# Renumbered column tiles and reordered products in a fused GEGLU feed-forward kernel

## The chip, the cores and the metric

The kernel runs on one core of a Trainium2 chip. The metric is device time in microseconds (us) of one execution. The kernel before took 276.17 us (median of 3 runs, 275.99 to 276.23).

Engines: PE is TensorE's matmul, PEld its weight load (it overlaps PE), DVE is VectorE, ACT is ScalarE, POOL is GpSimd, SP is SyncE, which here only issues transfers.

## The reference

```python
def _gelu(x):
    return jax.nn.gelu(x, approximate=True)

# x: (32, 32, 1024), w_gate and w_up: (1024, 3584), w_down: (3584, 1024), all bf16
def reference(x, w_gate, w_up, w_down):
    return (_gelu(x @ w_gate) * (x @ w_up)) @ w_down
```

As matrices: 1024 tokens, 1024 features, 3584 hidden columns, which are 28 column tiles of 128.

## The kernel before

The kernel lowers the number of matmuls with a seven-product scheme for 2 x 2 block matrices. The four blocks of the moving operand are halves of the tokens and halves of the contraction. The two column blocks of the weights are a "left" and a "right" tile, and there are 13 such pairs (two left-over tiles are computed directly at the start). Products 1 and 2 of a pair use plain weights and inputs (bf16). Products 3 to 7 use sums that DVE, POOL and ACT prepare, in fp32r; the profile prints their type as f32, and this text says fp32. A product is four matmuls of 128 x 512 for gate and four for up.

Four stages follow one another on PE:

- the start: 128 direct bf16 matmuls, fed by the first loads;
- four early pairs, whose products 1 and 2 were already done in the start, so each has 40 fp32 matmuls;
- nine later pairs, each with 16 bf16 and 40 fp32 matmuls;
- seven sweeps for the down projection, in the same scheme.

The program is a list of operations. PE keeps the order in which they are written. The other engines are sorted by the estimate `at`, and semaphores are added by dependence. One helper emits all operations, so nearly every operation has the same line in the profile (L117).

```python
        NX, F0 = 2, 11
        ...
        def load_first(eng, j, k0, k1, after=()):
            dma(eng, first[:, j, k0:k1, :], w_r[j][:, k0:k1, F0 * P:(F0 + 4) * P], 0, f"w0_{j}_{k0}", after)
        ...
        LEFT = [11, 12] + list(range(11))
        NP, EARLY = len(LEFT), 4

        def left(p): return LEFT[p]
        def right(p): return LEFT[p] + 15
        ...
        A, E, B, C = (0, 1), (2, 3), (4, 5), (6, 7)      # PSUM banks
        for p in range(NP):
            ...
            if p < EARLY:
                o = -4
                for j in range(2):
                    act(bank(B[j]), kept[p][:, j, :], COPY, at(0.1 + j * 0.1))
                product(5, 0, E[0], True)
                act(p5[0], bank(E[0]), COPY, at(1))
                product(5, 1, E[1], True)
                product(6, 0, B[0], False)
                act(bank(C[0]), bank(B[0]), COPY, at(3))
                act(p5[1], bank(E[1]), COPY, at(3.1))
                product(6, 1, B[1], False)
                act(bank(C[1]), bank(B[1]), COPY, at(4))
            else:
                o = 0
                product(1, 0, A[0], True)
                act(bank(B[0]), bank(A[0]), COPY, at(1))
                product(1, 1, A[1], True)
                act(bank(B[1]), bank(A[1]), COPY, at(2))
                product(5, 0, E[0], True)
                act(p5[0], bank(E[0]), COPY, at(3))
                product(2, 0, A[0], False)
                act(g11, bank(A[0]), GELU, at(4))
                product(2, 1, A[1], False)
                glu(ml, 0, g11, bank(A[1]), at(5.2))
                product(6, 0, B[0], False)
                act(bank(C[0]), bank(B[0]), COPY, at(6))
                product(6, 1, B[1], False)
                act(bank(C[1]), bank(B[1]), COPY, at(7))
                product(5, 1, E[1], True)
                act(p5[1], bank(E[1]), COPY, at(8))
            ...
            product(7, 0, C[0], False)        # adds to the copy in bank C
            ...
            product(3, 0, B[0], False)
            product(7, 1, C[1], False)
            product(3, 1, B[1], False)
            product(4, 0, C[0], False)
            product(4, 1, C[1], False)
```

`product(n, j, bank, start)` is half a product (j = 0 gate, j = 1 up), four matmuls of about 0.9 us together. In the text, "product 6" before "product 7" means these halves.

## Time and profile before

| stage, from the trace of before | us |
|---|---|
| up to the first fp32 matmul | 33.60 |
| early pairs (first to last matmul start) | 36.75 |
| later pairs (up to the last fp32 matmul start) | 113.46 |
| first two sweeps (bf16) | 24.23 |
| other sweeps, to the last matmul start | 63.45 |
| last matmul and stores | 3.25 |
| span | 274.73 |

The page of the profile says at once which engine to read. These are parts 1 and 4 of the page (busy time and share of the span; the chain of work that ended last) and two lines of part 5 (count, busy us, mean ns of one, idle time before):

```profile
span 274.7 us, 3245 instructions
PE 269.5 (98%) x1186; PEld 187.4 (68%) x1200; DVE 189.8 (69%) x221; ACT 126.1 (46%) x195; POOL 45.5 (17%) x27
...
PE 96%; DMA 2%; issue 0%; DVE 0%; ACTq 0%
...
L117 PEld LDWEIGHTS ps<-S,T 128*128 128x128 f32 x520 | 97.4, 188 | 22.7 <-issue 0.8
...
L117 PEld LDWEIGHTS ps<-arena 128*128 128x128 bf16 x272 | 24.7, 98 | 34.7 <-issue 4.5
```

PE is busy all the time and is the chain. "Busy" cannot show a small loss, since matmuls overlap (each is recorded as about 390 ns long, and the next starts after 216 or 227 ns); what counts is the distance from one matmul's start to the next. The trace has 1186 of 1200 matmuls here, so some blocks below read x7 for 8 or x15 for 16; the distance across a lost record is simply doubled. The instructions of PE in order of time, merged, show one later pair (start us, duration us, what):

```profile
96.01 1.67 PE L117 MATMUL ps<-arena 128*128 128x512 bf16 x7
97.34 1.27 PE L117 MATMUL ps<-S,T 128*128 128x512 f32 x4
98.45 1.90 PE L117 MATMUL ps<-arena 128*128 128x512 bf16 x8
100.00 8.55 PE L117 MATMUL ps<-S,T 128*128 128x512 f32 x36
108.62 1.67 PE L117 MATMUL ps<-arena 128*128 128x512 bf16 x7
```

The pair lasts 108.62 - 96.01 = 12.61 us, and goes from bf16 to fp32 twice. Single distances in the trace, in ns, around the second of these returns:

```
bf16 216, 217 | 27, 419, 229, 233, 236, 224, 231, 236, 228, 233, 231 | 226, 227, 227, 226
```

The steady distance is 216 ns for bf16 and 226.7 ns for fp32. The 27 and 419 belong together (the start of the first fp32 matmul is recorded early). After them nine matmuls are out of rhythm, 224 to 236 ns apart and on the whole late. Without such losses a pair would take 40 x 226.67 + 16 x 216 = 12,523 ns. It takes 12,607.

The early pairs lose in another way. ACT's instructions in order of time around the second early pair (the bracket gives idle time of ACT before, and what ended it):

```profile
44.88 0.58 ACT L117 ACTIVATE tmp<-ps 128x512 f32<-128x512 f32 x1
45.92 0.58 ACT L117 ACTIVATE ps<-ps 128x512 f32<-128x512 f32 x1 [0.46 <-PE ps L117]
46.42 0.59 ACT L117 ACTIVATE tmp<-ps 128x512 f32<-128x512 f32 x1
```

The middle line is the copy from bank B to bank C. It starts when product 6 ends and ends at 46.505 us; product 7's first matmul, which adds to the copy, starts at 46.650. The distances on PE there are 227, 226, 247, 306, 229, 233, 236 ns: 247 up to product 7's first matmul, 306 from it to the second. So PE is held up here in every early pair.

### The profile page before, as it was taken

To read this page: it belongs to the slowest core of one execution; us is meant where nothing else is said; L and a number is where in the kernel's file an instruction comes from. 1 tells how busy PE (TensorE), PEld (TensorE's weight loads), DVE (VectorE), ACT (ScalarE), POOL (GpSimd) and SP (SyncE) were. 2 spreads that over 40 slices of the span, in tenths; PEclk is the share of its full clock that TensorE was granted. 3 is DMA by queue.
4 is the path that set the end of the run, shared out by engine and by line. 5 is a ranking of instruction groups with operands and counts; after the bars stand their busy time and mean duration, and the time that the engine had idled before them with its cause. 6 is when DMAs were issued, how large, how long until landed. Compare 5 with 4: busy or idle time off the path is not lost.

```text
span 274.7 us, 3245 instructions
## 1 busy us (share of the span) xinstructions
PE 269.5 (98%) x1186; PEld 187.4 (68%) x1200; DVE 189.8 (69%) x221; ACT 126.1 (46%) x195; POOL 45.5 (17%) x27
## 2 busy tenths in 40 slices
PE   8999999999999999999999999999999999999995
PEld 4344478888686767767686867674447888888884
DVE  1039978988566657384655666579971999999942
ACT  2333766577455555556464555531120112255561
POOL 1000031134160605234150606000000000000000
PEclk9999999999999999999999999999999999999999
DMA  7999502962900830092500007097011000001112
GB/s 172 236 229 297 138 9 72 276 221 73 232 2 0 219 86 2 18 288 59 96 2 0 0 0 252 17 301 237 0 38 38 0 2 0 0 0 61 38 57 76
DMA packets 46863, 26.42 MB, mean 96 GB/s; under 512 B 12544, under 2 KB 46848, under 8 KB 46848
## 3 DMA queue, kind: packets, MB, share of 16 engines
q1 hardware_dynamic: 44624, 24.25, 32.5%
q10 hardware_dynamic: 2224, 1.97, 3.1%
q8 instruction: 9, 0.15, 0.2%
q14 instruction: 6, 0.05, 0.1%
HBM read 22.28 MB, written 2.10 MB: 89 GB/s over the span
## 4 chain that ended last, share of the span: by engine, by line
PE 96%; DMA 2%; issue 0%; DVE 0%; ACTq 0%
PE ps L117 96%; DMA arena<-in_w_up_dram 2%; DVE arena L117 0%; ACTq L117 0%
## 5 line engine op out<-in xcount | busy, mean ns | idle before, releaser
L117 PE MATMUL ps<-S,T 128*128 128x512 f32 x520 | 125.5, 398 | 0.0
L117 PEld LDWEIGHTS ps<-S,T 128*128 128x128 f32 x520 | 97.4, 188 | 22.7 <-issue 0.8
L117 POOL TENSOR_TENSOR T<-arena 128x1024 fp32r<-128x1024 bf16 x21 | 44.8, 2151 | 123.4 <-DVE T L117 114.7
L117 DVE TENSOR_TENSOR hT<-tmp,ps 128x512 bf16<-128x512 f32 x56 | 37.2, 686 | 39.2 <-PE ps L117 36.8
L117 ACT ACTIVATE tmp<-ps 128x512 f32<-128x512 f32 x64 | 38.2, 597 | 56.4 <-PE ps L117 56.4
L117 PE MATMUL ps<-arena 128*128 128x512 bf16 x261 | 60.7, 381 | 1.5 <-DMA arena<-in_w_up_dram 0.6
L117 ACT ACTIVATE ps<-ps 128x512 f32<-128x512 f32 x52 | 30.3, 584 | 48.4 <-PE ps L117 48.4
L117 PE MATMUL ps<-T,S 128*128 128x512 f32 x224 | 51.3, 390 | 0.0
L117 DVE TENSOR_TENSOR T<-arena,T 128x1024 fp32r<-128x1024 bf16 x40 | 48.5, 1219 | 0.0
L117 PEld LDWEIGHTS ps<-arena 128*128 128x128 bf16 x272 | 24.7, 98 | 34.7 <-issue 4.5
L117 PEld LDWEIGHTS ps<-T,S 128*128 128x128 f32 x224 | 42.1, 188 | 8.8
L117 DVE TENSOR_TENSOR tmp<-ps,tmp 128x512 f32<-128x512 f32 x26 | 18.0, 692 | 21.9 <-PE ps L117 21.9
L117 DVE TENSOR_TENSOR T<-arena 128x1024 fp32r<-128x1024 bf16 x19 | 22.7, 1222 | 7.5 <-PE ps L117 7.4
L117 PE MATMUL ps<-arena,hT 128*128 128x512 bf16 x109 | 24.0, 379 | 0.2
L117 DVE TENSOR_TENSOR ps<-ps,tmp 128x512 f32<-128x512 f32 x30 | 20.9, 696 | 2.8 <-PE ps L117 2.8
L117 PEld LDWEIGHTS ps<-arena,hT 128*128 128x128 bf16 x112 | 10.9, 98 | 13.2 <-issue 0.3
L117 ACT ACTIVATE tmp<-tmp 128x512 f32<-128x512 f32 x26 | 16.4, 632 | 5.8 <-DVE tmp L117 4.6
L117 DVE TENSOR_TENSOR S<-hT 128x1024 fp32r<-128x1024 bf16 x14 | 16.6, 1221 | 0.0
L117 ACT ACTIVATE T<-arena 128x1024 fp32r<-128x1024 bf16 x13 | 13.7, 1053 | 0.0
L117 PE MATMUL ps<-S 128*128 128x512 f32 x56 | 12.9, 389 | 0.0
L117 PEld LDWEIGHTS ps<-S 128*128 128x128 f32 x56 | 10.5, 188 | 2.2
L117 ACT ACTIVATE S<-arena 128x1024 fp32r<-128x1024 bf16 x9 | 9.3, 1056 | 3.1 <-PE ps L117 3.0
(25 smaller groups left out, 62.1 us busy)
## 6 DMA issues: line engine op xcount, KB each, us to landing
arena<-in_w_down_dram SPq DMA_DIRECT2D x4, 1792.0 KB, 9.3
arena<-in_w_gate_dram SPq DMA_DIRECT2D x10, 512.0 KB, 5.7
arena<-in_w_up_dram SPq DMA_DIRECT2D x10, 512.0 KB, 6.6
out_dram<-arena SPq DMA_DIRECT2D x12, 128.0 KB, 1.7
arena<-in_w_gate_dram SPq DMA_DIRECT2D x4, 256.0 KB, 4.9
arena<-in_w_up_dram SPq DMA_DIRECT2D x4, 256.0 KB, 5.0
arena<-in_w_up_dram ACTq DMA_DIRECT2D x4, 128.0 KB, 5.1
arena<-in_w_gate_dram ACTq DMA_DIRECT2D x2, 256.0 KB, 5.5
```

What stands on the lines that cost most here:

```text
L117: ins = name(eng, *args, **kw) if callable(name) else getattr(eng, name)(*args, **kw)
```

## The change

The intent: all weight transfers should begin at multiples of 512 bytes, and the second products (product 2) of a pair should run last, next to the first products of the following pair, so that bf16 matmuls stand together. The early pairs get a new order as well.

```diff
-        NX, F0 = 2, 11
+        NX = 2
-            dma(eng, first[...], w_r[j][:, k0:k1, F0 * P:(F0 + 4) * P], ...)
+            dma(eng, first[...], w_r[j][:, k0:k1, 0:4 * P], ...)
-        LEFT = [11, 12] + list(range(11))
+        LEFT = [2, 3] + list(range(4, 14)) + [14]
+        RIGHT = [26, 27] + list(range(16, 26)) + [15]
-        def right(p): return LEFT[p] + 15
+        def right(p): return RIGHT[p]
...      (tile indices follow; the last pair, tiles 14 and 15, is loaded with two transfers, not four;
...       the estimates behind `at`, which sort the other engines, are adjusted)
-        A, E, B, C = (0, 1), (2, 3), (4, 5), (6, 7)
+        B, C = (4, 5), (6, 7)
         for p in range(NP):
+            short, last = p < EARLY, p == NP - 1
+            A, E = ((0, 1), (2, 3)) if short or (p - EARLY) % 2 == 0 else ((2, 3), (0, 1))
...
+            def second(at_):
+                product(2, 0, A[0], False)
+                act(g11, bank(A[0]), GELU, at_ + 0.95 * SLOT)
+                product(2, 1, A[1], False)
+                glu(ml, 0, g11, bank(A[1]), at_ + 2.2 * SLOT)
...      (the two branches shown above become one:)
+            o = 4 if short else 7.8 if last else 5.9
+            if short:
+                for j in range(2):
+                    act(bank(B[j]), kept[p][:, j, :], COPY, at(0.1 + j * 0.1))
+            else:
+                for j in range(2):
+                    product(1, j, A[j], True)
+                    move(A[j], B[j], at(0.95 * (j + 1)))
+            product(5, 0, E[0], True)
+            act(p5[0], bank(E[0]), COPY, at(o - 3))
+            if last:
+                second(at(2.9))
+            product(6, 0, B[0], False)
+            move(B[0], C[0], at(o - 2))
+            if short:
+                product(5, 1, E[1], True)
+            product(6, 1, B[1], False)
+            move(B[1], C[1], at(o - 1))
+            if not short:
+                product(5, 1, E[1], True)
+            act(p5[1], bank(E[1]), COPY, at(o - 0.9))
             ...  (products 7, 3, 7, 3, 4, 4 as before)
+            if not short and not last:
+                second(at(o + 6))
```

In an early pair the halves now run 5, 6, 5, 6, 7 ... instead of 5, 5, 6, 6, 7 ... . In a later pair they run 1, 1, 5, 6, 6, 5, 7, 3, 7, 3, 4, 4, 2, 2. Number and shapes of all matmuls stay the same.

More of the change, by code (lines that the diff above doesn't have):

```diff
@@ L208, in load_first @@
         def load_first(eng, j, k0, k1, after=()):
-            dma(eng, first[:, j, k0:k1, :], w_r[j][:, k0:k1, F0 * P:(F0 + 4) * P], 0, f"w0_{j}_{k0}", after)
+            dma(eng, first[:, j, k0:k1, :], w_r[j][:, k0:k1, 0:4 * P], 0, f"w0_{j}_{k0}", after)
         def load_x(h, k0, k1, after=()):
@@ L229, in bass_standalone__geglu_ffn__sampling_kernel @@
                 pr.add("dve", "tensor_copy", xT[0][:, k, i * 256:(i + 1) * 256], half)
-        LEFT = [11, 12] + list(range(11))
+        LEFT = [2, 3] + list(range(4, 14)) + [14]
+        RIGHT = [26, 27] + list(range(16, 26)) + [15]
         NP, EARLY = len(LEFT), 4
         def left(p): return LEFT[p]
-        def right(p): return LEFT[p] + 15
+        def right(p): return RIGHT[p]
         kept = [hT[:, m:m + 2, :].rearrange("p t n -> p (t n)").bitcast(FP32).rearrange("p (j n) -> p j n", j=2)
-                for m in (7, 9, 22, 24)]
-        SLOT = 0.905
-        t0 = 32.7
+                for m in (10, 12, 22, 24)]
+        SLOT = 0.9064
+        t0 = 33.0
         T0 = []
@@ L248, in bass_standalone__geglu_ffn__sampling_kernel @@
             T0.append(t0)
-            t0 += (10 if p < EARLY else 13.9) * SLOT
+            t0 += (10 if p < EARLY else 13.84) * SLOT
         base = t0
@@ L256, in bass_standalone__geglu_ffn__sampling_kernel @@
             steps += [(m, j, k) for j in range(2) for k in range(DK - KO, DK)] + [(m, None, None)]
+        tile = lambda m: (m + 2) % 4
         for m, j, k in steps:
@@ L260, in bass_standalone__geglu_ffn__sampling_kernel @@
                 act(tmp[:, m, :], bank(2 * m), GELU, at)
-                tt(hT[:, F0 + m, 0:512], tmp[:, m, :], bank(2 * m + 1), MUL, at)
+                tt(hT[:, tile(m), 0:512], tmp[:, m, :], bank(2 * m + 1), MUL, at)
                 continue
-            op = mm(2 * m + j, first[:, j, k, m * P:(m + 1) * P], xT[0][:, k, :], k == 0, k in (3, DK - 1), add=k > 3)
+            op = mm(2 * m + j, first[:, j, k, tile(m) * P:(tile(m) + 1) * P], xT[0][:, k, :], k == 0, k in (3, DK - 1), add=k > 3)
             if k == 3 and m < 2:
@@ L281, in bass_standalone__geglu_ffn__sampling_kernel @@
                 act(tmp[:, m, :], bank(2 * m), GELU, at)
-                tt(hT[:, F0 + 2 + m, 512:1024], tmp[:, m, :], bank(2 * m + 1), MUL, at)
+                tt(hT[:, m, 512:1024], tmp[:, m, :], bank(2 * m + 1), MUL, at)
                 continue
-            mm(2 * m + j, first[:, j, k, (m + 2) * P:(m + 3) * P], xT[1][:, k, :], k == 0, k == DK - 1)
+            mm(2 * m + j, first[:, j, k, m * P:(m + 1) * P], xT[1][:, k, :], k == 0, k == DK - 1)
         def load_near(at):
@@ L291, in load_pairs @@
         def load_pairs(gi, s, at, ks=slice(0, DK)):
-            n = min(2, NP - 2 * gi)
             for j in range(2):
                 m = (left, right)[s](2 * gi)
-                dma("sp", raw[gi % 2][:, s, j, ks, 0:n * P], w_r[j][:, ks, m * P:(m + n) * P], at, f"w{gi}_{j}{s}_{ks.start}")
+                dma("sp", raw[gi % 2][:, s, j, ks, :], w_r[j][:, ks, m * P:(m + 2) * P], at, f"w{gi}_{j}{s}_{ks.start}")
         load_near(10)
@@ L308, in pair_w @@
             if p < 2:
-                return first[:, :, ks, col] if s == 0 else near[:, :, ks, col]
+                return first[:, :, ks, slice((p + 2) * P, (p + 3) * P)] if s == 0 else near[:, :, ks, col]
+            if p == NP - 1:
+                return raw[0][:, 0, :, ks, slice(s * P, (s + 1) * P)]
             return raw[(p // 2) % 2][:, s, :, ks, col]
@@ L367, in bass_standalone__geglu_ffn__sampling_kernel @@
         t4 = sums_w(0, 4, 33.9)
-        A, E, B, C = (0, 1), (2, 3), (4, 5), (6, 7)
+        B, C = (4, 5), (6, 7)
         for p in range(NP):
             t0 = T0[p]
+            short, last = p < EARLY, p == NP - 1
+            A, E = ((0, 1), (2, 3)) if short or (p - EARLY) % 2 == 0 else ((2, 3), (0, 1))
             if p % 2 == 0 and 2 <= p // 2 + 1 < (NP + 1) // 2:
                 load_pairs(p // 2 + 1, 0, t0)
-                load_pairs(p // 2 + 1, 1, t0)
+                if p < NP - 3:
+                    load_pairs(p // 2 + 1, 1, t0)
             if p == 3:
                 load_wd(0, 0, t0)
-            if p == NP - 1:
+            if last:
                 load_wd(0, 1, t0)
@@ L390, in product, with move @@
                     mm(b, l, r, start and k == 0, k == 3, add=not start)
+            def move(a, b, at_):
+                act(bank(b), bank(a), COPY, at_)
             def glu(m, h, g, u, at_):
                 tt(hT[:, m, h * 512:(h + 1) * 512], g, u, MUL, at_)
+            def second(at_):
[3 more added lines that the diff above has]
+                glu(ml, 0, g11, bank(A[1]), at_ + 2.2 * SLOT)
@@ L395, in bass_standalone__geglu_ffn__sampling_kernel @@
             p5 = [tmp[:, 0, :], tmp[:, 1, :]]
             g11, g12, g22, g21 = (tmp[:, i, :] for i in range(2, 6))
-            if p < EARLY:
-                o = -4
+            o = 4 if short else 7.8 if last else 5.9
+            if short:
                 for j in range(2):
                     act(bank(B[j]), kept[p][:, j, :], COPY, at(0.1 + j * 0.1))
-                product(5, 0, E[0], True)
-                act(p5[0], bank(E[0]), COPY, at(1))
-                product(5, 1, E[1], True)
-                product(6, 0, B[0], False)
-                act(bank(C[0]), bank(B[0]), COPY, at(3))
-                act(p5[1], bank(E[1]), COPY, at(3.1))
-                product(6, 1, B[1], False)
-                act(bank(C[1]), bank(B[1]), COPY, at(4))
-            else:
-                o = 0
-                product(1, 0, A[0], True)
-                act(bank(B[0]), bank(A[0]), COPY, at(1))
-                product(1, 1, A[1], True)
-                act(bank(B[1]), bank(A[1]), COPY, at(2))
-                product(5, 0, E[0], True)
-                act(p5[0], bank(E[0]), COPY, at(3))
-                product(2, 0, A[0], False)
-                act(g11, bank(A[0]), GELU, at(4))
-                product(2, 1, A[1], False)
-                glu(ml, 0, g11, bank(A[1]), at(5.2))
-                product(6, 0, B[0], False)
-                act(bank(C[0]), bank(B[0]), COPY, at(6))
-                product(6, 1, B[1], False)
-                act(bank(C[1]), bank(B[1]), COPY, at(7))
@@ new lines, in bass_standalone__geglu_ffn__sampling_kernel @@
+            else:
[4 more added lines that the diff above has]
+            act(p5[0], bank(E[0]), COPY, at(o - 3))
+            if last:
+                second(at(2.9))
+            product(6, 0, B[0], False)
+            move(B[0], C[0], at(o - 2))
+            if short:
+                product(5, 1, E[1], True)
+            product(6, 1, B[1], False)
+            move(B[1], C[1], at(o - 1))
@@ L426, in bass_standalone__geglu_ffn__sampling_kernel @@
+            if not short:
                 product(5, 1, E[1], True)
-                act(p5[1], bank(E[1]), COPY, at(8))
+            act(p5[1], bank(E[1]), COPY, at(o - 0.9))
             u22 = bank(A[1] if p < EARLY - 1 else E[1])
             product(7, 0, C[0], False)
-            tt(g22, bank(C[0]), p5[0], ADD, at(o + 9.1))
-            act(g22, g22, GELU, at(o + 10))
+            tt(g22, bank(C[0]), p5[0], ADD, at(o + 1.1))
+            act(g22, g22, GELU, at(o + 2))
             product(3, 0, B[0], False)
-            tt(g12, bank(B[0]), p5[0], ADD, at(o + 10.1))
@@ L434, in bass_standalone__geglu_ffn__sampling_kernel @@
-            act(g12, g12, GELU, at(o + 11))
+            tt(g12, bank(B[0]), p5[0], ADD, at(o + 2.1))
+            act(g12, g12, GELU, at(o + 3))
             product(7, 1, C[1], False)
-            tt(u22, bank(C[1]), p5[1], ADD, at(o + 11.1))
-            glu(mr, 1, g22, u22, at(o + 11.9))
+            tt(u22, bank(C[1]), p5[1], ADD, at(o + 3.1))
+            glu(mr, 1, g22, u22, at(o + 3.9))
             product(3, 1, B[1], False)
-            tt(bank(B[1]), bank(B[1]), p5[1], ADD, at(o + 12.1))
@@ L440, in bass_standalone__geglu_ffn__sampling_kernel @@
-            glu(mr, 0, g12, bank(B[1]), at(o + 13))
+            tt(bank(B[1]), bank(B[1]), p5[1], ADD, at(o + 4.1))
+            glu(mr, 0, g12, bank(B[1]), at(o + 5))
             product(4, 0, C[0], False)
-            act(g21, bank(C[0]), GELU, at(o + 13))
+            act(g21, bank(C[0]), GELU, at(o + 5))
             product(4, 1, C[1], False)
-            glu(ml, 1, g21, bank(C[1]), at(o + 14.1))
-            if p + 1 < NP:
-                sums_w(p + 1, 0, at(o + 9), "pool", [t4])
+            glu(ml, 1, g21, bank(C[1]), at(o + 6.1))
@@ L447, in bass_standalone__geglu_ffn__sampling_kernel @@
+            if not short and not last:
+                second(at(o + 6))
+            if not last:
+                sums_w(p + 1, 0, at(o + 1), "pool", [t4])
                 if p + 1 < EARLY:
-                    sums_w(p + 1, 1, at(o + 11.5))
-                    sums_w(p + 1, 2, at(o + 14.3))
-                    sums_w(p + 1, 3, at(o + 9.5))
-                    t4 = sums_w(p + 1, 4, at(o + 14.4))
-                else:
-                    sums_w(p + 1, 1, at(o + 14.3))
-                    sums_w(p + 1, 2, at(o + 12), "pool")
-                    sums_w(p + 1, 3, at(o + 9.5))
-                    t4 = sums_w(p + 1, 4, at(o + 20.5))
+                    sums_w(p + 1, 1, at(o + 3.5))
+                    sums_w(p + 1, 2, at(o + 6.3))
+                    sums_w(p + 1, 3, at(o + 1.5))
+                    t4 = sums_w(p + 1, 4, at(o + 6.4))
+                else:
+                    sums_w(p + 1, 1, at(o + 6.3))
+                    sums_w(p + 1, 2, at(o + 4), "pool")
+                    sums_w(p + 1, 3, at(o + 1.5))
+                    t4 = sums_w(p + 1, 4, T0[p + 1] + 4.4 * SLOT)
```

## The prediction

> **What bounds the kernel.** TensorE's instruction stream. The page gives PE 269.5 of 274.7 us (98%), and the chain of waits is 96% PE; only one matmul wait (0.6 us) and one weight-load wait (1.0 us) are on a transfer, before 14 us. DVE (69%), ACT (46%), POOL (17%) and later transfers are off the chain. Number and shapes of matmuls do not change, so only the spacing of their starts can win (instructions in order of time).
>
> **Where spacing is lost.** Steady spacing is 227 ns for fp32, 216 ns for bf16.
> - Each of the nine later pairs takes 12.607 us; ideal is 40 x 226.7 + 16 x 216 = 12.523, so 84 ns are lost. The loss sits where bf16 and fp32 meet: going to bf16 costs about 22 ns, and the first nine or so fp32 starts afterwards are 229 to 236 ns apart. Weight loads take 188 ns (fp32) and 98 ns (bf16); that agrees with the Trainium skill, "TensorE: Matmul & The Clock Gate", section "Weight-path perf modes": fast weight load is not for fp32. A pair has two such round trips: one of 4 fp32 matmuls (26 ns lost), one of 36 (59 ns).
> - Each of the four early pairs loses 115 to 140 ns: at its 16th and 17th matmul the spacing is 246 and 306 ns. There product 7 waits for ACT's 0.58 us copy of the bank that product 6 finished only one product (0.9 us) earlier.
>
> **What the change does.**
> 1. Second products at a pair's end, beside the next pair's first: 16 bf16 together, then 40 fp32. One round trip less in 8 of 9 pairs. Estimate: 8 x 26 = 0.21 us; pair 12.607 -> 12.58 us.
> 2. In early pairs product 6 runs second, so the copy has two products' time. Estimate: four stalls of some 115 ns vanish, 0.45 us; pairs 9.20 -> 9.07 to 9.10 us.
> 3. Alignment: I expect nothing. Landings follow each other 1.78 us apart for 512 KB from aligned starts, 1.63 to 1.93 us from odd multiples of 256 B; packets take 33 ns in both. The Trainium skill, "DMA: Bandwidth & Descriptors", section "How a descriptor splits into AXI transactions", puts the break at 256 B, which the old starts already met; the trace agrees. The last pair's four transfers of 256-byte runs become two of 512-byte runs, off the chain. The first loads feed the one real stall (0.7 us near 13 us), which may move by some tenths either way.
> 4. New dependences (moves before product 6, GELU of the second product before its bank's reuse) have at least a product of slack over ACT's 0.6 us. The last down-weight transfers still land near 191 us, needed at 196.
>
> **Prediction.** 276.17 - 0.21 - 0.45 = 275.5 us; range 274.7 to 276.2. Faster by over 2%: 0.01; within 2%: 0.97; slower by over 2%: 0.02.
>
> **Right or wrong in the profile.** Later pairs at 12.58 us, each with one run of 16 bf16 starts; early pairs without the 306 ns spacing; packets still near 33 ns; first fp32 product starting at 33.6 +/- 0.3 us; the final sweeps (from 184 us) only shifted.
>
> **What would make it wrong.** A new wait of PE on ACT's moves at product 6 or on a reused bank, in every pair; a changed start because of transfer order; DVE, full from 184 to 200 us, delaying the third sweep's preparation; a longer fp32 recovery after 16 bf16 than after 8.

## The result, and the profile after

The changed kernel took 274.88 us (median of 5 runs, 274.54 to 275.21), against 275.99 for the kernel before in the same rounds (275.17 to 276.23). The ratio is 0.9968, with a 95% interval of 0.9947 to 0.9988. Ratios here are computed as the mean time of one kernel's fast runs over that of the other's of the same rounds, so they are not quite the ratio of the medians quoted. By the limit of 2% the verdict is "same", but the gain is clear of noise.

```profile
span 272.7 us, 3266 instructions
PE 268.1 (98%) x1186; PEld 188.1 (69%) x1200; DVE 189.2 (69%) x221; ACT 125.7 (46%) x195; POOL 45.4 (17%) x27
...
PE 98%; issue 0%; DVE 0%
...
L117 PEld LDWEIGHTS ps<-S,T 128*128 128x128 f32 x520 | 97.7, 188 | 21.3
...
L117 PEld LDWEIGHTS ps<-arena 128*128 128x128 bf16 x272 | 25.1, 98 | 33.4 <-issue 3.4
```

This page (the same parts as before) tells little of where 2 us of span went: PE is still 98% busy and its weight loads take the same 188 and 98 ns. Only the 2% of the chain that were a wait for a transfer ("DMA 2%") are gone, which points at the start. The same view of PE in order of time tells more:

```profile
92.54 3.40 PE L117 MATMUL ps<-arena 128*128 128x512 bf16 x15
95.59 9.44 PE L117 MATMUL ps<-S,T 128*128 128x512 f32 x40
105.10 2.11 PE L117 MATMUL ps<-arena 128*128 128x512 bf16 x9
```

There is one block of 16 bf16 matmuls (one record is lost) and one of 40 fp32, and the pair lasts 105.10 - 92.54 = 12.56 us. After the return to fp32 six matmuls are out of rhythm, not nine:

```
bf16 216, 216 | 28, 418, 224, 231, 236, 228, 232, 231 | 227, 227, 226, 227
```

In the second early pair, ACT's view now reads:

```profile
44.07 0.59 ACT L117 ACTIVATE ps<-ps 128x512 f32<-128x512 f32 x1
45.55 0.58 ACT L117 ACTIVATE ps<-ps 128x512 f32<-128x512 f32 x1 [0.88 <-PE ps L117]
46.04 0.59 ACT L117 ACTIVATE tmp<-ps 128x512 f32<-128x512 f32 x1
```

The first line is the copy to bank C that product 7 needs. It ends near 44.66 us, and product 7 starts at 45.347: the copy is done about 0.7 us early, and the distances on PE stay at 227 ns. An early pair went from 9.18 to 9.21 us (second and third pair) to 9.07.

By stage, the two profiled runs differ so:

| stage, us | before | after | difference |
|---|---|---|---|
| up to the first fp32 matmul | 33.60 | 32.42 | -1.18 |
| early pairs | 36.75 | 36.28 | -0.47 |
| later pairs | 113.46 | 113.09 | -0.37 |
| the rest | 90.93 | 90.96 | +0.03 |
| span | 274.73 | 272.74 | -1.99 |

The early and later pairs moved about as foreseen. The largest single difference is in the start, where nothing was foreseen but the alignment of the loads had been changed. So the first question for the chip was: is that 1.18 us a gain from alignment, or chance?

### The profile page after: what moved, and what is told of

The parts are those of the page before. It is cut to its first block, busy times and chain, and to the rows that moved or that the text cites. A ratio compares the mean times of both kernels' runs of the same rounds, so it can differ in the third digit from the quotient of the medians.

```text
span 272.7 us, 3266 instructions
## 1 busy us (share of the span) xinstructions
PE 268.1 (98%) x1186; PEld 188.1 (69%) x1200; DVE 189.2 (69%) x221; ACT 125.7 (46%) x195; POOL 45.4 (17%) x27
## 4 chain that ended last, share of the span: by engine, by line
PE 98%; issue 0%; DVE 0%
PE ps L117 98%; DVE arena L117 0%
## 5 line engine op out<-in xcount | busy, mean ns | idle before, releaser
L117 PE MATMUL ps<-S,T 128*128 128x512 f32 x520 | 122.0, 393 | 0.0
L117 PE MATMUL ps<-arena 128*128 128x512 bf16 x261 | 59.0, 379 | 0.8
L117 PE MATMUL ps<-S 128*128 128x512 f32 x56 | 12.9, 389 | 0.0
```

Of the source, the lines that this page charges most:

```text
L117: ins = name(eng, *args, **kw) if callable(name) else getattr(eng, name)(*args, **kw)
```

## The experiments

Eleven runs were made, two of them repeats of the two kernels shown above. Runs on one chip share the runs of the kernel before: the first four (276.29 us, 11 runs), the next four (276.22 us), the last three (276.34 us).

### First group: which half of the change carries the gain?

**align_only**: the kernel before with the new numbering alone; the order of instructions on PE is that of before.

```diff
-        LEFT = [11, 12] + list(range(11))
+        LEFT = [2, 3] + list(range(4, 14)) + [14]
+        RIGHT = [26, 27] + list(range(16, 26)) + [15]
...      (first loads from column 0, and the tile indices that follow; products as in before)
```

> Only the new numbering of the column tiles, with the order of products of the kernel before. Theory A (alignment is worth nothing, the faster start of the profiled run is chance): first fp32 product at 33.6 +/- 0.3 us, later pairs 12.607 us, early pairs as before, time within 0.2 us of before. Rival B (aligned starts speed up the first loads): first fp32 product near 32.4 us and time about 1.0 to 1.2 us below before, the rest unchanged.

Measured: 276.17 us, ratio to before 0.9999 (0.9983 to 1.0015), result correct. Later pairs 113.46 us in sum and early pairs 36.71, both as before. In the profiled run the first fp32 matmul was at 32.74 us, which theory A had not allowed; but the timed runs show no gain at all. One look and six timed runs disagree, so the start needed more looks.

**order_only**: the whole change with the old numbering.

```diff
-        LEFT = [2, 3] + list(range(4, 14)) + [14]
-        RIGHT = [26, 27] + list(range(16, 26)) + [15]
+        LEFT = [11, 12] + list(range(11))
...      (right tile = left tile + 15, first loads from tile 11, four loads for the last pair)
```

> The old numbering of tiles with the new order of products. Theory A: all of the change's gain that is not chance is here: early pairs 0.47 us less in sum, later pairs 12.560 us each (0.37 us less in sum), time 0.8 us below before, first fp32 product where before has it. Rival B: the same stage times, but the start stays at about 33.6 us, and the whole change beats this by about 1 us on the same chip.

Measured: 275.05 us, ratio 0.9954 (0.9940 to 0.9969), correct. Early pairs 36.25 us, later pairs 113.09, the first fp32 matmul at 33.18. All of the gain in the two pair stages is here without alignment.

**first_shift_256**: the whole change, with only the first loads moved by one tile (256 bytes); wrong result.

```diff
-            dma(eng, first[:, j, k0:k1, :], w_r[j][:, k0:k1, 0:4 * P], ...)
+            dma(eng, first[:, j, k0:k1, :], w_r[j][:, k0:k1, P:5 * P], ...)
```

> The whole change, but the first weight loads (8 transfers of 1 KB runs) read one tile further on, so they begin at an odd multiple of 256 bytes; wrong result on purpose, nothing else differs. Theory A: start and time as the whole change, within 0.2 us. Rival B: first fp32 product about 1 us later, time about 1 us above the whole change.

Measured: 275.60 us, ratio 0.9977 (0.9961 to 0.9993). The profiled run had its first fp32 matmul at 33.90 us. **whole_again**, the change itself on this chip:

> The whole change again, on this chip, for the other three to be compared with. Theory A: same as order_only within 0.2 us, ratio to before 0.997. Rival B: faster than order_only and first_shift_256 by about 1 us.

Measured: 275.31 us, ratio 0.9963 (0.9947 to 0.9980), correct, first fp32 matmul at 32.98 us. The shifted kernel is 0.3 us slower than this one, order_only is 0.3 us faster than it, and both of those have unaligned first loads. (Theory A had 0.2 us for both differences; they have opposite signs, and the three intervals overlap.) So the timed runs give no sign of a 1 us gain from alignment. The profiled starts still did: three aligned ones at 32.42, 32.74 and 32.98 us, three unaligned ones at 33.60, 33.18 and 33.90.

The traces say what differs in these starts. Weight loads in order of time in order_only, from the eight transposes on:

```profile
3.46 0.83 PEld L117 LDWEIGHTS ps<-ident,hT 128*128 128x128 bf16 x8
4.58 0.14 PEld L117 LDWEIGHTS ps<-arena 128*128 128x128 bf16 x2 [0.29 <-issue]
4.99 0.15 PEld L117 LDWEIGHTS ps<-arena 128*128 128x128 bf16 x1 [0.28 <-DVE arena L117]
5.42 0.15 PEld L117 LDWEIGHTS ps<-arena 128*128 128x128 bf16 x1 [0.28 <-issue]
5.84 0.15 PEld L117 LDWEIGHTS ps<-arena 128*128 128x128 bf16 x1 [0.28 <-issue]
6.27 0.15 PEld L117 LDWEIGHTS ps<-arena 128*128 128x128 bf16 x1 [0.28 <-issue]
6.70 2.31 PEld L117 LDWEIGHTS ps<-arena 128*128 128x128 bf16 x11 [0.28 <-issue]
```

Up to 6.7 us the loads stand alone, 0.42 us apart: the matmuls run at half rate, 427 ns each instead of 216. Only then do they merge. The Trainium skill, "TensorE: Matmul & The Clock Gate", section "Part 1: The HAM clock gate", says that the array starts at half its clock, and that the window which releases it is free-running and does not restart with the kernel. The trace agrees with the two rates (427 and 216 ns). If that is so, how many real matmuls fall into the slow part is chance and not the kernel's doing. That is a guess about these six looks until the same kernel is looked at twice.

### Second group: the start again, and each of the two losses enlarged

**before_again**: the kernel before, unchanged.

> The kernel before against itself: ratio 1.000, the noise of such a comparison; and a second look at its start. Theory A (the start's length is chance: how many of the first real matmuls still run at 427 ns, and one stall on a load): first fp32 product anywhere between 32.4 and 34 us, with another number of 427 ns matmuls than the 2 of the first look. Rival B (alignment): again 33.6 us with a stall of 0.7 us near 13 us.

Measured: 275.92 us, ratio to its own other runs 1.0000 (0.9979 to 1.0021). The first fp32 matmul was at **32.25 us**, earlier than in any other trace (and than the 32.4 us that theory A had as its limit), with unaligned loads. No real matmul ran at half rate, and after 5 us no distance in the start was over 284 ns. The same view of its weight loads:

```profile
3.75 0.55 PEld L117 LDWEIGHTS ps<-ident,hT 128*128 128x128 bf16 x8 [0.31 <-DMA hT<-in_x_dram]
4.69 4.23 PEld L117 LDWEIGHTS ps<-arena 128*128 128x128 bf16 x21 [0.40 <-DMA arena<-in_w_gate_dram]
```

From 4.69 us on the loads are merged in one row of 21.

**before_first_0**: the kernel before, with its first loads aligned; wrong result.

```diff
-            dma(eng, first[...], w_r[j][:, k0:k1, F0 * P:(F0 + 4) * P], ...)
+            dma(eng, first[...], w_r[j][:, k0:k1, 0:4 * P], ...)
```

> The kernel before, but its first weight loads read from column 0 (aligned to 512 bytes) instead of column 1408; wrong result on purpose. Theory A: ratio to before 1.000 within 0.0015. Rival B: about 0.8 us faster (ratio 0.997), first fp32 product near 32.6 us, no stall on the up weights near 12 us.

Measured: 276.18 us, ratio 1.0002 (0.9986 to 1.0018), first fp32 matmul at **33.78 us** with aligned loads. Rival B falls: aligned starts in the traces lie between 32.4 and 33.8 us, unaligned ones between 32.2 and 33.9. What goes with a late start differs between executions:

| run | first loads | time lost to half rate, us | largest later gap between matmuls | first fp32, us |
|---|---|---|---|---|
| before | unaligned | 0.43 | 937 ns at 12.9 us | 33.60 |
| before_again | unaligned | 0.00 | 284 ns | 32.25 |
| order_only | unaligned | 1.06 | 294 ns | 33.18 |
| first_shift_256 | unaligned | 0.95 | 948 ns at 12.3 us | 33.90 |
| after | aligned | 0.04 | 320 ns, and two across a lost record | 32.42 |
| align_only | aligned | 0.10 | 434 ns at 7.9 us | 32.74 |
| whole_again | aligned | 0.00 | 927 ns at 25.2 us | 32.98 |
| before_first_0 | aligned | 0.87 | 512 ns at 12.4 us | 33.78 |

(Time lost to half rate is the sum, over the real matmuls before 7.4 us, of what their distance exceeds 216 ns by, at most 211 ns each.) Both parts appear with either alignment.

The record holds more on this than the views show. The packed traces of all runs but first_shift_256 and second_first hold the time at which the full clock was granted (no view prints it): 3.39 us in whole_again, 3.66 in before_again, 4.74 in after, 4.84 in align_only, 5.53 in before, 6.62 in before_first_0, 6.79 in order_only. The two looks at one kernel differ by 1.9 us (before) and 1.3 us (the change). The first real matmul starts at 4.6 to 4.8 us, and half the time from there to the release gives the third column within 0.04 us (and nothing where the release came first). The timed runs can be used too: in the four traces with the old order of products the time after the first fp32 matmul is 241.11 to 241.21 us, so the span of each timed run less this is an estimate of its start. It is 33.1 us on average for the kernel before (33 runs, from 32.4 to 33.9), and 33.1 us for both align_only and before_first_0 (6 runs each). So the alignment moves the start by nothing that can be seen, and chance moves it by 1.5 us.

**early_no_gap**: the suspected wait of the early pairs doubled and more. Product 7 runs right after the half of product 6 whose copy it needs.

```diff
             product(5, 0, E[0], True)
+            if short: product(5, 1, E[1], True)
             product(6, 0, B[0], False)
             move(B[0], C[0], ...)
-            if short:
-                product(5, 1, E[1], True)
+            if short:
+                product(7, 0, C[0], False)
             product(6, 1, B[1], False)
             move(B[1], C[1], ...)
...      (the estimates at, which only sort ACT and DVE, follow)
```

> The whole change, but in the four early pairs product 7 runs right after product 6, so PE must wait for ACT's copy of the bank between them with no product to cover it. Theory (the early loss is that wait): a stall of about 0.9 us per early pair before product 7 and another of about 0.1 us before the second product 7, early stage about 40.5 us instead of 36.5, time about 4 us above the whole change (ratio to before 1.011). Rival (the early loss is a rhythm of the fp32 matmuls, not a wait): early stage unchanged within 0.5 us.

Measured: 279.47 us, ratio 1.0120 (1.0102 to 1.0139), correct; early pairs 40.56 us, later pairs 113.09. In each early pair the distances are 1151 ns up to product 7's first matmul and 308 ns from it to the second, and 261 ns after the first matmul of its second half (for this last one a stall of 0.1 us had been expected). The waits of PE within 34 to 69 us (us in total, times, longest) appear only here:

```profile
PE ps L117 <- ACT ps L117: 2.3, 3, 0.8
PE ps L117 <- DVE T L117: 0.8, 1, 0.8
```

The fourth is put down to DVE, but each gap has the same length and order. ACT's view of the second one shows it:

```profile
44.77 1.07 ACT L117 ACTIVATE tmp<-ps 128x512 f32<-128x512 f32 x2
45.81 0.58 ACT L117 ACTIVATE ps<-ps 128x512 f32<-128x512 f32 x1
```

Here the last matmul of product 6 starts at 45.389 us and is recorded as 388 ns long (the ends of matmuls are modelled in this profile); ACT's copy starts 37 ns after its end, takes 582 ns, and product 7 starts 144 ns after that. The sum is 388 + 37 + 582 + 144 = 1151 ns. In the kernel before, the same way from product 6 to product 7 was 1153 ns (45.497 to 46.650 us), while the matmuls between would have taken only 5 x 226.7 = 1134 ns. So PE missed the copy by some 20 ns. With the change nine distances, 2040 ns, lie between. The rival falls.

The miss of 20 ns costs more than 20 ns: the next distance is 306 instead of 227 (in early_no_gap 308), and the matmuls after it are some ns late again. Together an early pair lost 9.18 to 9.21 - 9.07 = 0.11 to 0.14 us.

**split_second**: in the later pairs the two halves of product 2 stand apart, so there are three returns from bf16 to fp32.

```diff
             product(5, 0, E[0], True)
+            if not short: product(2, 0, A[0], False)
             product(6, 0, B[0], False)
+            if not short: product(2, 1, A[1], False)
             product(6, 1, B[1], False)
...      (the last pair's own `second(at(2.9))` is taken out; GELU, product with it and estimates follow)
-            if not short and not last:
-                second(at(o + 6))
```

> The early pairs as changed; in each later pair the two second products stand apart (one after product 5, one after product 6), so there are three visits to fp32 instead of one. Theory (each return from bf16 to fp32 costs 26 to 59 ns): pairs of about 12.63 to 12.65 us instead of 12.560, later stage 0.7 to 0.8 us longer than with the change. Rival (what counts is the distance of a product from the copy it needs): pairs at 12.56 to 12.61 us.

Measured: 275.70 us, ratio 0.9983 (0.9965 to 1.0001), correct; later pairs 113.70 us, which is 12.633 us each and 0.61 us more than with the change (the text had 0.7 to 0.8 for this difference; its 12.63 to 12.65 for one pair is met). PE in order of time:

```profile
94.74 1.90 PE L117 MATMUL ps<-arena 128*128 128x512 bf16 x8
96.29 1.27 PE L117 MATMUL ps<-S,T 128*128 128x512 f32 x4
97.40 1.04 PE L117 MATMUL ps<-arena 128*128 128x512 bf16 x4
98.09 1.28 PE L117 MATMUL ps<-S,T 128*128 128x512 f32 x4
99.21 1.04 PE L117 MATMUL ps<-arena 128*128 128x512 bf16 x4
99.89 7.41 PE L117 MATMUL ps<-S,T 128*128 128x512 f32 x31
```

PE waits for nothing here; the additional loss comes with the additional returns. It is not the same for each of them: in this pair the two short fp32 blocks lose 27 and 36 ns, and the long one is back in rhythm after six matmuls (28, 420, 231, 231, 236, 228, 233, 230, then 227).

### Third group: is it the pair's border, and is the early gain its own?

**second_first**: as the change, but product 2 follows product 1 in its own pair.

```diff
+            if not short:
+                second(at(1.9))
             product(5, 0, E[0], True)
...      (an estimate follows)
-            if last:
-                second(at(2.9))
...
-            if not short and not last:
-                second(at(o + 6))
```

> The early pairs as changed; in each later pair the second products follow the first ones of the same pair at once (order 1, 1, 2, 2, 5, 6, 6, 5, 7 ...), so 16 bf16 matmuls still stand together but nothing crosses into the next pair. Theory (only the number of returns from bf16 to fp32 counts): pairs at 12.560 us as with the change, the last pair too, so the later stage lasts 113.04 us or a little less, against 113.09 with the change and 113.46 before. Rival (crossing into the next pair is what pays, or PE now waits for ACT's copy of the first product before the second overwrites it): pairs at 12.60 us or more.

Measured: 274.77 us, ratio 0.9946 (0.9930 to 0.9963), correct; later pairs 113.040 us. PE in order of time:

```profile
94.29 3.63 PE L117 MATMUL ps<-arena 128*128 128x512 bf16 x16
97.56 9.44 PE L117 MATMUL ps<-S,T 128*128 128x512 f32 x40
106.85 0.39 PE L117 MATMUL ps<-arena 128*128 128x512 bf16 x1
```

A pair again takes 106.85 - 94.29 = 12.56 us. Nothing about the border between pairs pays; sixteen bf16 matmuls in one block do. This order is a little simpler and is 0.05 us shorter in the stage than the change, because the last pair too has one block. In time it cannot be told from the change (both intervals to before overlap); it is the fastest kernel here by a margin that the runs do not prove.

**early_old**: the whole change with the early pairs in the old order 5, 5, 6, 6, 7.

```diff
             product(5, 0, E[0], True)
+            if short:
+                product(5, 1, E[1], True)
             product(6, 0, B[0], False)
-            if short:
-                product(5, 1, E[1], True)
             product(6, 1, B[1], False)
...      (the estimates of the copies follow)
```

> The whole change, but the four early pairs have their products in the old order (5, 5, 6, 6, 7). Theory: early stage 36.7 to 36.8 us as before instead of 36.25 to 36.28, with the spacings of about 245 and 310 ns back in each early pair; later stage 113.09 us; ratio to before about 0.9986. Rival (the early gain comes from what else the change does): early stage stays under 36.4 us.

Measured: 275.68 us, ratio 0.9985 (0.9964 to 1.0006), correct; early pairs 36.73 us with distances of 245 and 312 ns back in each pair, later pairs 113.09. The early gain comes from the order of these four products alone.

**first_shift_128**: the whole change, with the first loads 128 bytes past an aligned column (one look, no timed rounds, so of unknown state); wrong result on purpose.

```diff
-            dma(eng, first[...], w_r[j][:, k0:k1, 0:4 * P], ...)
+            dma(eng, first[...], w_r[j][:, k0:k1, 64:64 + 4 * P], ...)
```

> The whole change, but the first weight loads begin 128 bytes past an aligned column, so no longer at a multiple of 256 bytes; wrong result on purpose. If the break is at 256 bytes: the median packet of 1 KB among the first loads takes longer than the 46 ns seen with all starts so far[...]. If start alignment costs nothing at all: 46 ns again.

Measured: 275.19 us in its single run. Among the 2048 first packets of 1 KB the median took 46 ns and the fastest tenth 46 ns too, the same as in each kernel with aligned or half-aligned starts. No cost of the start's alignment was seen even here.

## Why the prediction was right, point by point

- **The bound.** It held: PE is the chain before (96%) and after (98%), and each gain came from the distances of matmul starts.
- **Early pairs, 0.45 us.** Right in mechanism and size: 0.47 us in the profiled pair of runs. early_no_gap shows that the wait is ACT's copy, early_old that the order of the four products undoes it. The prediction took the whole 115 to 140 ns as a wait; the wait proper is only about 20 ns. The rest comes in the matmuls right after it and is gone where the wait is gone; why an interruption costs that much is open.
- **Later pairs, 0.21 us.** Right in mechanism, too small in size: 0.37 us. The term mis-sized is "8 x 26". The prediction charged the removed return with the loss inside its own four-matmul block (26 ns), and left the long block at 59 ns. Measured, a pair falls from 12.607 to 12.560 us, 47 ns: besides the short block's loss, the recovery in the long block is shorter (six matmuls out of rhythm, not nine), where the prediction had named a longer one as a risk. Then 8 x 47 = 0.37 us. Against the ideal 12.523, one, two and three returns in a pair lose 37, 84 and 110 ns (second_first and the change, before, split_second). What sets the length of the recovery is open: it is not the missing short block alone, for in split_second it is six although two short blocks come first. A fixed price for each return is therefore not shown.
- **Alignment, nothing.** Right as far as the runs can tell: align_only 0.9999 and before_first_0 1.0002, each to about 0.16% (0.44 us). Packets of the later loads, between 64 and 76 us, have a median of 32 ns before and after. A gain of some tenths of a us is not excluded by these ratios; one of 1 us is. The estimated starts, 33.1 us with either alignment, say the same.
- **The start, 33.6 +/- 0.3 us.** Wrong as a statement about one look: it was 32.42 us. The prediction held only "tenths" of chance there, while starts of 32.25 to 33.90 us were seen without any relation to the kernel. It had listed the one 0.7 us stall but not the half-rate matmuls, which alone make up to 1.06 us.
- **The time.** Predicted 275.5 us (274.7 to 276.2), measured 274.88. The gain that stays, read from the stages, is 0.47 + 0.37 = 0.84 us, against 0.66 predicted. The ratio of 0.9968 is 0.88 us of 276. That leaves 0.62 us between 275.5 and 274.88: 0.18 us because the gain was larger, 0.18 us because the starting point, 276.17 us, was the median of three runs and five runs gave 275.99, and about 0.3 us that no stage explains and that is less than the chance of the start. That the figure stayed within the range, 0.18 us from its lower end, is in part luck.
- **New dependences.** None of them held PE up: in 34 to 69 us and in the later pairs PE waits for nothing after the change, and the later stage has the same length to 1 ns in after, order_only, early_no_gap and early_old (113.086 to 113.087 us). The last down-projection weights landed at 189.6 us (foreseen: near 191), and the bf16 sweeps that use them lasted 24.23 us as before.

## What to carry to other kernels

When PE is the chain and 98% busy, compare the distances between matmul starts with their steady value, and do this by stage: a pair of 12.607 us against an ideal of 12.523 shows a loss that no busy share does. Put matmuls of one type in one block (37 ns lost per pair with one block, 84 with two, 110 with three), and let at least two products, as halves of four matmuls are called here, lie between a product and the one that needs a copy of its bank; here a copy that came 20 ns late cost over 100 ns. Before reading a difference in the first 34 us as a gain, look at the same kernel twice: here the profiled start moved by more than the change was worth.

## What the Trainium skill lacked or had wrong

- "TensorE: Matmul & The Clock Gate", Part 1: it gives about +/- 500 ns for where the clock is released. Here the packed traces put the release at 3.39 us (whole_again) to 6.79 us (order_only), a spread of 3.4 us, which moves a 276 us kernel by up to 1.06 us. The same Part does say elsewhere that one kernel showed 6, 11 or 14 slow matmuls in different runs. The page of the profile prints a granted clock of 9 tenths or more in the first slices also where matmuls are 427 ns apart, so the half rate is not seen there.
- The same page has no cost for going between bf16 and fp32 weights. Measured: one, two and three returns to fp32 in a pair lose 37, 84 and 110 ns, and in the long block six to nine matmuls are 224 to 236 ns apart before the steady 226.7.
- The same page gives about 216 ns for back-to-back matmuls of 512 columns, which the bf16 ones meet (216 ns). It has no figure for fp32r: measured 226.7 ns, with a weight load of 188 ns.
- No page that I found has the time from one product through an ACT copy to the next product in PSUM: 1151 ns from start to start for 128 x 512 (388 + 37 + 582 + 144, of which the 388 is modelled).
- "DMA: Bandwidth & Descriptors", section "How a descriptor splits into AXI transactions": by its rule, a transaction starts at a multiple of 256 bytes, so a 1 KB run that starts 128 bytes off one takes five transactions instead of four (an estimate worked out from the page). A 1 KB packet 128 bytes off took the same median of 46 ns, so in this kernel that cost was not visible.
